# A fused attention and gated-MLP kernel: new order at the front, at the switch and at the tail, and a halved score tile ordered through VectorE with its second half earlier

## The chip, the cores and the metric

The kernel runs on one core of a Trainium2 chip. The metric is the device time of one execution in microseconds, the median of several. The engines named below are TensorE (PE; its weight loads are PEld), VectorE (DVE), ScalarE (ACT), GpSimd (POOL) and SyncE (SP, which issues DMAs); each has its own queue of instructions and runs it in order.

## What is computed

`x` is 2048 tokens of 512 features. It is normalised (layer norm without weights). An attention block with 32 heads of 16 features and an MLP with a hidden width of 1376 both read the normalised `x`; the MLP's result, through silu, gates the attention's result, and `x` is added.

```python
def _A_ref(x, wqkv, wo):                       # H = 32, Dh = 16
    qkv = (x @ wqkv).reshape(B, S, 3, H, Dh).transpose(2, 0, 3, 1, 4)
    q, k, v = qkv[0], qkv[1], qkv[2]
    p = softmax(einsum("bhqd,bhkd->bhqk", q, k) * Dh ** -0.5)
    o = einsum("bhqk,bhkd->bhqd", p, v)
    return o.transpose(0, 2, 1, 3).reshape(B, S, D) @ wo
def _B_ref(x, w1, b1, w2, b2):
    return gelu(x @ w1 + b1) @ w2 + b2
xn = layernorm(x)
return x + _A_ref(xn, wqkv, wo) * silu(_B_ref(xn, w1, b1, w2, b2))
```

## The kernel before

**Precision.** Most matmuls run on a rounded format (float32r) and take operands as a high part and a remainder (low part). A product is then three matmuls, high by high, high by low, low by high (`mm3`, L80).

**Row tiles.** The array is used as two row tiles of 64 rows, which run matmuls side by side. One score matmul needs 48 or 50 rows. The kernel never lets both row tiles write one PSUM bank at once: where both write one bank, the second waits until the first has finished.

**Units and heads.** The 32 heads form 8 groups of 4; the tokens form 4 chunks of 512. A unit is one group and one chunk of queries, 32 units in all. Attention runs in two passes. The first finds, per query, the maximum over a group's scores: score matmuls of 128 queries by 512 keys (L183, function `s_mm`) and reductions on VectorE (`s_max`, L189). The second makes scores again, transposed (`t_one`, L732), with the maximum folded in, ScalarE takes the exponential (L734), and the result is multiplied by V and a column of ones (`pv_step`, L797; 8 matmuls, as float32).

**Stages.** At the front (to about 57 us), tokens are loaded, normalised (`ln`: `moments`, `rstd`, `norm`; L418 to L432), transposed and split into high and low (`turn`, `split`, L74 and L75); V and the first two groups of queries and keys follow (`v_tile`, `q_first`). Then, to about 480 us, a plan interleaves the MLP and the other queries and keys (`quad`, `half`, `down`; `quad` makes four V tiles, `half` one row tile's share of two products) with score matmuls of the first pass (`fill`). From there on, a loop over n = 0 to 512 runs both passes: at each n an order string is read, one letter after the other:

- T: one transposed score matmul of the second pass with its exponential; four in each n.
- S: one whole score tile (128 by 512) of the first pass, with its reduction. Successive S take alternate row tiles.
- X and Y: a halved tile. X computes 256 keys of one head on the first row tile into the first half of a bank; Y computes 256 keys of another head on the second row tile into the other half of the same bank; then one reduction covers both. So X and Y must not overlap, and Y's matmul waits for a token.
- V: the eight matmuls of `pv_step` for the step before.

The token is an empty instruction on an engine's queue: it waits for X's matmul, and Y waits for it.

```python
token = nc.gpsimd.nop().ins                                               # L221
tc.add_manual_dep(token, x.name, SYNC, reason="row tile done")
...
tc.add_manual_dep(y, token.name, SYNC, reason="other row tile")
```

Waits are counts on semaphores: a waiting instruction names an engine and how many of its counted instructions must have finished. An instruction that waits holds up those behind it on its queue.

The order is `ORDER[3]` where three score tiles fall due in a step, which is 490 steps in a row; `ORDER[0]` ("TTTTV") where none does. n = 0 and n = 1 have strings of their own. Score tiles of the first pass take three PSUM banks in turn (`s_ring`); X holds its bank until Y's reduction has been asked for (`s_ring.append(pool)` in `s_op`), and a matmul into a bank waits for the reduction that read it last. T takes four other banks in turn, V one.

After the loop comes the tail: the last unit is divided by its sums (`o_move`, `o_den`, `o_div`), token tiles are rounded (`w_token`, `w_chunk`, `w_round`), multiplied by `wo` (`w_mul`, L80), gated and added (`w_gate` L893, `w_add` L898) and stored. T3 are the last four token tiles, 12 to 15; tile 15 is done in two halves of 256 columns.

Of the kernel before, what the change touches and what calls it, by code (L numbers as in the profile page):

```python
# [16 lines left out]
P = 128  # L17
# [19 lines left out]
FILL0 = 38  # L37
HB = 4
W2B = 2
ORDER = {0: "TTTTV", 3: "TXSTTSTYV"}  # L40
HC = CH // 2
PAIRED = 28
KB = 3
# [5 lines left out]
def fused(ctx: ExitStack, tc: tile.TileContext, x, wqk, wv, wo, w1, b1, w2, b2, out):  # L49
# [27 lines left out]
    def mm3(ps, lhs, rhs, first, last, then=None):  # L77
        n = 0
        for a, b in ((0, 0), (0, 1), (1, 0)):
            nc.tensor.matmul(ps, lhs[a], rhs[b], start=first and n == 0, stop=last and n == 2)  # L80
            n += 1
            if then:
                then()
# [42 lines left out]
    def slot(i, shape, dtype=F32):  # L126
        return big.tile(list(shape), dtype, name=f"slot{i}")
# [81 lines left out]
    def s_op(op):  # L209
        if op == "S":  # L210
            if whole:
                s_whole(whole.pop(), 1)
            else:
                whole.append(jobs.pop(0))
                s_whole(whole[0], 0)
        elif op == "X":
            if not cut:
                cut[:] = [jobs.pop(0), 0]
            ps, pool = s_tile(True)
            x = s_mm(ps, cut[0], 0, 0, cut[1] * HC, HC)  # L220
            token = nc.gpsimd.nop().ins  # L221
            tc.add_manual_dep(token, x.name, SYNC, reason="row tile done")
            cut[2:] = [ps, pool, token]
            run_off()
        else:
            job, n, ps, pool, token = cut
            y = s_mm(ps, job, 1, HC, n * HC, HC)
            tc.add_manual_dep(y, token.name, SYNC, reason="other row tile")
            s_max(ps, job, slice(0, 2), n)
            s_ring.append(pool)  # L230
            cut[1] += 1
            if n:
                cut.clear()
# [76 lines left out]
            pairs.append([("q", g, c), ("q", g, c + 1)])  # L310
    parts = [(c, f, h) for c in range(NCH) for f in range(FT) for h in range(2)]
    is_m = [pair[0][0] == "m" for pair in pairs]
    plan, nd = [("first", g) for g in range(VQ - 1)], 0
    for j in range(len(pairs)):
        for h in range(2):
            plan.append(("half", j, h))
            if j == 0 and h == 1:
                plan.append(("first", VQ - 1))
            ready = 4 * sum(is_m[:j])
            due = next((i for i in range(j, len(pairs)) if is_m[i]), len(pairs))  # L320
            nxt = next((i for i in range(j + h, len(pairs)) if is_m[i]), len(pairs))
            left = 2 * (nxt - j) + 1 - h
            need = 4 * sum(is_m[:nxt]) - 4 - nd
            room = 2 * (due + 1 - j) - h
            n = 2 if nd < len(parts) and parts[nd][2] and ready - nd > room else 1
            n = max(n, need - 2 * (left - 1))
            while nd < ready and n > 0:
                c, f, k = parts[nd]
                if f == 0 and k == 0 and plan[-1][0] == "down":
                    break  # L330
                plan.append(("down", parts[nd]))
                nd += 1
                n -= 1
# [58 lines left out]
    with ExitStack() as s1:  # L392
# [4 lines left out]
        def a_tile(shape):  # L397
            banks[0] += 1
            i = banks[0] % 6
            if i < 3:  # L400
                return (ps_a, ps_b, ps_x)[i].tile(list(shape), F32, name="ps")
            return ps_t.tile(list(shape), F32, name="pst")
# [48 lines left out]

        def q_first(c):
            pq = {}
            for g in range(2):
                ps = pq["q", g, c] = a_tile((P, CH))
                for k in range(KT):
                    ks = slice(k * P, (k + 1) * P)
                    mm3(ps, (W1[g][0][:, ks], W1[g][1][:, ks]), (xh[c][:, k], xl[c][:, k]), k == 0, k == KT - 1)
            evac(list(pq), pq)

        for t in range(4):
# [39 lines left out]
        def wv_low(k):  # L501
            nc.gpsimd.tensor_sub(wv_l[:, k], wv_r[:, k], wv_h[:, k].bitcast(F32))
# [5 lines left out]
            turn(t)  # L508
        for k in range(KT):
            nc.scalar.activation(wv_h[:, k], wv_r[:, k], AF.Copy)  # L510
        for k in range(KT - 1):
            wv_low(k)
        ln(NCH, NCH)
        consts()
        pool_after(2 * NCH - 1)
        wv_low(KT - 1)
        q_first(0)
        for c in range(1, NCH):
            for t in range(NCH * c, NCH * c + NCH):
# [21 lines left out]
        qzs.append(qzp.tile([P, 2, CH], F32R, name=f"qz{i}"))  # L541

    load_qs(0)
    load_k(0, c0=0, n=S - CH)
    v_tile(NCH - 2)
    q_first(NCH - 1)
    v_tile(NCH - 1)
# [144 lines left out]
            run((terms(y, 0, False), terms(x, 1, False)), {2: [lambda: w1_load(j + 2), errand], 10: [chore]})  # L692
            evac((x, y), PH)

    def quad(n):
        us = first[n]
        for u, b in zip(us, BANKS[n]):
            pool, name = {"x": (ps_x, "ps"), "m": (ps_m, "ps"), "v": (ps_v, "pv"), "t": (ps_t, "pst")}[b]
            PH[u] = pool.tile([P, CH], F32, name=name)
        for i in range(4):  # L700
            hooks = {6: [mark]} if i in (1, 2) else {}
            if n == VQ - 2 and i in (0, 2):
                hooks[3] = [lambda: w1_split(0) if i == 0 else w1_load(1)]
            run((terms(us[i], 0, i < 2), terms(us[(i + 2) % 4], 1, i < 2)), hooks)
            if i >= 2:
                for u in (us[i - 2], us[i]):
                    v_out(u[1] * NCH + u[2], PH.pop(u))
# [29 lines left out]
    for n, e in enumerate(plan):  # L737
        if e[0] == "half":
            half(*e[1:])
        elif e[0] == "first":  # L740
            quad(e[1])
            if e[1] == 0:
                ask_qs(1)
        else:
            if e[1] == parts[-2]:
                nc.scalar.activation(mhw, ident_r[:1, :1].bitcast(F32), AF.Exp)
            if e[1] == parts[-1]:
                for i in range(EARLY):
                    t_one(0, 0, i // 2, i % 2)
            down(*e[1])  # L750
        if e == ("first", VQ - 1):
            w2_split(0)
            w2_load(2)
            ask_k(1)
        if e[0] == "half" and pairs[e[1]][0] == ("q", NG - 1, 0) and e[2] == 1:
            kts.append([slot(p, (P, S), F32R) for p in range(2)])
            kws.append(None)
            qss.append(slot(2, (P, 2, 2, CH), F32R))
            ask_k(2)
        if n == len(plan) - 8:  # L760
            load_qt(0)
            load_mh(0)
# [46 lines left out]
    def o_rows(u, j):  # L809
        g, c = divmod(u, NCH)  # L810
        r0 = 64 * (g % 2) + DH * j
        return slice(r0, r0 + DH), c, g // 2
# [10 lines left out]
    def o_den(u):  # L823
        dr = DR.pop(u)
        nc.vector.reciprocal(dr, dr)
        nc.sync.dma_start(den_d[u].rearrange("j (a i) -> (j a) i", i=GH * CH // P), dr)
        DN[u] = wb.tile([P, CH], F32, name="dn", bufs=1)
        for j in range(GH):
            nc.sync.dma_start(DN[u][o_rows(u, j)[0]], den_d[u, j:j + 1].to_broadcast([DH, CH]))

    def o_div(u, eng):
        g, c = divmod(u, NCH)
# [25 lines left out]
        nc.vector.scalar_tensor_tensor(g, e, 1.0, g, op0=OP.add, op1=OP.mult)  # L858

    def w_round(blocks, src, lo):  # L860
        oh = wb.tile([P, KT, P], F32R, name="oh", bufs=3)
        ol = wb.tile([P, KT, P], F32R, name="ol", bufs=3)
        n = len(blocks)
        nc.scalar.activation(oh[:, :n], src, AF.Copy)
        lo.tensor_sub(ol[:, :n], src, oh[:, :n].bitcast(F32))
        for i, b in enumerate(blocks):
            OTS[b] = (oh[:, i], ol[:, i])
# [28 lines left out]
    def w_add(t, eng, i=0):  # L896
        gx, cs = GX[t], cols(t)[i]
        eng.tensor_add(gx[:, 0, cs], gx[:, 0, cs], gx[:, 1, cs])  # L898
        nc.sync.dma_start(out[t * P:(t + 1) * P, cs], gx[:, 0, cs])

    def w_out(t, eng):
        w_gate(t)
        w_add(t, eng)
# [50 lines left out]
    for n in range(L + 1):  # L954
        ua, ka = divmod(n, 16)
        want = due(n) - due(n - 1)
        i = 0
        for op in ORDER[want] if n > 1 else ("TTTTV", "TTTVTSS")[n]:
            if op in "SXY":
                s_op(op)  # L960
            elif op == "V":
                if n:
                    pv_step(*divmod(n - 1, 16))
                for _ in range(4):
                    tick()
                flush()
            else:
                if EARLY <= 4 * n + i < 4 * L:
                    t_one(ua, ka, i % 2, 1 - i // 2)
                for f, args in todo.get((n, i), []):  # L970
                    f(*args)
                i += 1
# [4 lines left out]
    w_out(late[0], nc.gpsimd)  # L977
    w_chunk(1, nc.gpsimd)
    w_mul(late[1], KS)
    w_out(late[1], nc.gpsimd)  # L980
    w_chunk(2, nc.gpsimd)
    for k in KS[:-1]:
        for t in T3:
            w_mul(t, (k,))
    o_div(NU - 1, nc.vector)
    w_chunk(KT - 1, nc.vector)
    ends = [(t, i) for t in T3 for i in range(len(cols(t)))]
    for n, (t, i) in enumerate(ends):
        w_mul(t, KS[-1:], (i,))
        w_gate(t, i)  # L990
        if n == 0:
            w_add(t, nc.gpsimd)
        elif n > 1:
            w_add(*ends[n - 1][:1], nc.vector, ends[n - 1][1])
    w_add(ends[-1][0], nc.vector, ends[-1][1])


# [31 lines left out]
```

## Time and profile before

| | |
|---|---|
| three runs | 1602.58, 1604.39, 1605.58 us |
| median | 1604.39 us |
| profiled execution, its own time | 1603.36 us |
| its span in the profile | 1601.6 us |
| instructions in it | 32363 |

The profile is of one execution. Times in it are microseconds from the start of the span unless marked ns. A row of the time line has the start, the length, the engine, the line of the kernel, the operation, what is written and read, the shapes, how many like it were merged (x3), and in brackets how long the engine was idle before and what ended that. A "q" behind an engine is its sequencer: waits and DMA issues, which do not count as busy time. Ends of matmuls are modelled. Line numbers are those of the kernel before; behind the change they are up to five higher.

### The profile page before, as it was taken

The numbers are of one execution on the slowest core, as the hardware profiler recorded it, in microseconds if no ns is written. First come the engines' busy times: TensorE is split into PE (matmuls) and PEld (weight loads), VectorE is DVE, ScalarE is ACT, GpSimd is POOL, SyncE is SP. The second block draws the span as 40 slices with busy tenths as digits, with TensorE's granted clock in tenths as the row PEclk, the third lists the DMA queues.
The fourth block names the chain that finished last, engine by engine and source line by source line (L and its number), as shares of the span: only waits on it lengthen the run. The fifth ranks groups of instructions, "written<-read, shape, count | busy, mean of one in ns | idle before, by whom it ended". The sixth has DMA issues, their size and how long they took to land.

```text
span 1601.6 us, 32363 instructions
## 1 busy us (share of the span) xinstructions
PE 1590.1 (99%) x12132; PEld 914.8 (57%) x12132; DVE 1380.9 (86%) x2257; ACT 1260.4 (79%) x2521; POOL 377.7 (24%) x398
## 2 busy tenths in 40 slices
PE   9999999999999999999999999999999999999998
PEld 7889899999994444444444444444444444444445
DVE  7489898989888999999999989999999999999743
ACT  4333443434349999999999999999999999999984
POOL 4135575756640001000100200100010000000144
PEclk9999999999999999999999999999999999999999
DMA  6625343454331113111410311321141111110252
GB/s 204 149 58 149 118 136 97 152 142 134 113 98 55 40 31 68 29 37 42 80 32 25 69 41 29 60 40 28 31 73 27 31 29 39 32 30 21 62 199 89
DMA packets 76286, 116.92 MB, mean 73 GB/s; under 512 B 24836, under 2 KB 26116, under 8 KB 74952
## 3 DMA queue, kind: packets, MB, share of 16 engines
q1 hardware_dynamic: 72668, 102.42, 22.7%
q0 software_dynamic: 3264, 12.35, 3.9%
q8 instruction: 96, 1.57, 0.4%
q14 instruction: 62, 0.51, 0.1%
q10 hardware_dynamic: 196, 0.07, 0.0%
HBM read 84.35 MB, written 25.97 MB: 69 GB/s over the span
## 4 chain that ended last, share of the span: by engine, by line
PE 97%; DVE 1%; DMA 0%; ACT 0%; issue 0%; SPq 0%; DVEq 0%; ACTq 0%
PE pv L797 32%; PE ps L183 18%; PE pst L732 16%; PE ps L583 12%; PE pst L583 7%; PE ps L732 5%; PE ps L80 3%; PE pv L583 2%; PE pst L80 1%; DVE slot L75 0%; DMA xt<-in_x 0%; DVE st L418 0%; DVE xn L432 0%; DVE slot L893 0%; ACT hh L377 0%
## 5 line engine op out<-in xcount | busy, mean ns | idle before, releaser
L189 DVE TENSOR_REDUCE mx<-ps 128x2 f32<-128x512 f32 x2048 | 1299.1, 685 | 152.9 <-PE ps L183 87.6
L734 ACT ACTIVATE slot<-pst 128x512 f32<-128x512 f32 x1533 | 833.8, 612 | 22.1 <-PE ps L732 8.9
L797 PE MATMUL pv<-slot,vsb 128*32 128x512 f32 x4096 | 545.3, 605 | 0.0
L183 PE MATMUL ps<-kt,slot 48*128 48x512 f32 (+1 forms) x1364 | 393.4, 376 | 0.0
L732 PE MATMUL pst<-qt,kt 50*128 50x512 f32 x1149 | 372.8, 430 | 0.5 <-DVE gt L665 0.4
L732 PEld LDWEIGHTS pst<-qt,kt 50*128 50x128 f32 x1149 | 178.9, 184 | 279.7 <-ACT slot L734 264.0
L734 ACT ACTIVATE slot<-ps 128x512 f32<-128x512 f32 x515 | 315.3, 613 | 4.4 <-PE ps L732 1.2
L183 PEld LDWEIGHTS ps<-kt,slot 48*128 48x128 f32 x1364 | 210.8, 184 | 34.7 <-DVE mx L189 22.1
L583 PE MATMUL ps<-slot,w1h 64*128 64x512 f32 x1088 | 218.5, 393 | 0.4 <-ACT junk L597 0.4
L183 PE MATMUL ps<-kt,qz 48*128 48x512 f32 x512 | 213.0, 416 | 0.0
L183 PE MATMUL ps<-slot,slot 48*128 48x512 f32 (+1 forms) x598 | 172.5, 376 | 0.7 <-DVE mx L189 0.7
L732 PE MATMUL ps<-qt,kt 50*128 50x512 f32 x387 | 162.4, 422 | 0.0
L583 PEld LDWEIGHTS ps<-slot,w1h 64*128 64x128 f32 x1088 | 152.1, 185 | 7.4 <-ACT junk L597 1.7
L797 PEld LDWEIGHTS pv<-slot,vsb 128*32 128x32 f32 x4096 | 80.6, 108 | 120.3 <-issue 112.2
L583 PE MATMUL ps<-slot,w1l 64*128 64x512 f32 x544 | 142.3, 393 | 0.0
L378 POOL TENSOR_TENSOR hl<-hg,hh 128x512 fp32r<-128x512 f32 x76 | 96.8, 1295 | 121.5 <-ACT hh L377 84.7
L597 ACT ACTIVATE junk<-ident_r 1x1 f32<-1x1 f32 x93 | 18.2, 196 | 124.8 <-PE pst L583 120.2
L732 PE MATMUL pst<-qt,slot 50*128 50x512 f32 x384 | 112.6, 416 | 0.0
L251 POOL CAST nmh<-nm 128x16 fp32r<-128x16 f32 x32 | 6.3, 197 | 414.6 <-PE ps L183 111.5
L183 PEld LDWEIGHTS ps<-kt,qz 48*128 48x128 f32 x512 | 93.7, 183 | 16.5 <-issue 0.4
L183 PEld LDWEIGHTS ps<-slot,slot 48*128 48x128 f32 x598 | 92.2, 184 | 17.1 <-DVE mx L189 11.4
L732 PEld LDWEIGHTS ps<-qt,kt 50*128 50x128 f32 x387 | 71.0, 184 | 44.0 <-ACT slot L734 42.8
(150 smaller groups left out, 1711.1 us busy)
## 6 DMA issues: line engine op xcount, KB each, us to landing
raw<-in_w SPq DMA_DIRECT2D x88, 256.0 KB
qk_h<-hh SPq DMA_DIRECT2D x32, 256.0 KB
qk_l<-hl SPq DMA_DIRECT2D x32, 256.0 KB
qt<-qk_h SPq DMA_DIRECT2D x128, 64.0 KB
slot<-qk_h SPq DMA_DIRECT2D x92, 64.0 KB
xt<-in_x SPq DMA_DIRECT2D x16, 256.0 KB
g_d<-gt POOLq DMA_DIRECT2D x16, 256.0 KB, 3.4
qt<-qk_l SPq DMA_DIRECT2D x64, 64.0 KB
```

The source lines that it names most:

```text
L80: nc.tensor.matmul(ps, lhs[a], rhs[b], start=first and n == 0, stop=last and n == 2)
L183: return nc.tensor.matmul(ps[:, c0:c0 + w], QS[u][r, p, qi * P:(qi + 1) * P], kts[u // NCH % KB][p][r, k0:k0 + w], start=True, stop=True).ins
L189: nc.vector.tensor_reduce(MX[u][:, 2 * p:2 * p + 2, qi, ki][:, heads, parts], ps.rearrange("p (n c) -> p n c", c=HC), axis=AX.X, op=OP.max)
L251: nc.gpsimd.tensor_copy(hl[:, 0], nm)
L378: nc.gpsimd.tensor_sub(hl, raw, hh.bitcast(F32))
L583: i = nc.tensor.matmul(ps, lhs[r], rhs[r], start=first, stop=last).ins
L597: i = nc.scalar.activation(junk[:, :1], ident_r[:1, :1].bitcast(F32), AF.Copy).ins
L732: nc.tensor.matmul(ps, kts[g % KB][p][r, k * P:(k + 1) * P], QT[u][r, p, :], start=True, stop=True)
L734: nc.scalar.activation(PT[u, k][:, 2 * p + a, :], ps, AF.Exp, scale=SCALE)
L797: nc.tensor.matmul(PV[u][32 * j:32 * j + 32, :], vsb[:, k, h:h + 32], PT[u, k][:, j, :], start=(k == 0), stop=(k == NT - 1))
```

## The change

Front: `q_first` runs all high-by-high products of its two groups first, then high by low part of x, then low part of the weights. The last two of four subtractions for the low part of V's weights (`wv_low`, on POOL) come after the second `ln` instead of the last one. The first load of K takes columns 0 to 511 and then 512 to 1535 instead of all 1536 at once. The third quad is cut in two and stands around the second half of the first pair.

Switch: the string for n = 1 is "TTSTSVT" instead of "TTTVTSS".

The step: the empty instruction is on VectorE's queue instead of POOL's, and the order string of a step with three tiles has Y ahead of the second S and of the last T.

Tail: the sums of a unit come back in one broadcast load instead of four; the last rounding has a buffer of its own; tile 15 is multiplied as a whole at the very end; all last adds are on VectorE.

```diff
-ORDER = {0: "TTTTV", 3: "TXSTTSTYV"}
+ORDER = {0: "TTTTV", 3: "TXSTTYTSV"}
...
-            token = nc.gpsimd.nop().ins
+            token = nc.vector.nop().ins
...
-    plan, nd = [("first", g) for g in range(VQ - 1)], 0
+    plan, nd = [("first", g, i) for g in range(VQ - 1) for i in (0, 2)], 0
...
-            if j == 0 and h == 1:
-                plan.append(("first", VQ - 1))
+            if j == 0:
+                plan.append(("first", VQ - 1, 2 * h))
...
-            for g in range(2):
-                ps = pq["q", g, c] = a_tile((P, CH))
-                for k in range(KT):
-                    ks = slice(k * P, (k + 1) * P)
-                    mm3(ps, (W1[g][0][:, ks], W1[g][1][:, ks]), (xh[c][:, k], xl[c][:, k]), k == 0, k == KT - 1)
+            for n, (i, j) in enumerate(((0, 0), (0, 1), (1, 0))):
+                for g in range(2):
+                    if n == 0:
+                        pq["q", g, c] = a_tile((P, CH))
+                    for k in range(KT):
+                        nc.tensor.matmul(pq["q", g, c], W1[g][i][:, k * P:(k + 1) * P], (xh, xl)[j][c][:, k],
+                                         start=n == 0 and k == 0, stop=n == 2 and k == KT - 1)
...
-        for k in range(KT - 1):
+        for k in range(KT - 2):
             wv_low(k)
         ln(NCH, NCH)
         consts()
         pool_after(2 * NCH - 1)
-        wv_low(KT - 1)
+        for k in range(KT - 2, KT):
+            wv_low(k)
...
-    load_k(0, c0=0, n=S - CH)
+    load_k(0, c0=0, n=CH)
+    load_k(0, c0=CH, n=S - 2 * CH)
...
-        for j in range(GH):
-            nc.sync.dma_start(DN[u][o_rows(u, j)[0]], den_d[u, j:j + 1].to_broadcast([DH, CH]))
+        r0 = o_rows(u, 0)[0].start
+        nc.sync.dma_start(DN[u][r0:r0 + GH * DH],
+                          den_d[u].rearrange("j (o c) -> j o c", o=1).to_broadcast([GH, DH, CH]))
...
+        if blocks == [(t, KT - 1) for t in T3]:
+            both = slot(3 + len(PN) % 3, (P, 4, KT, P), F32R)
+            oh, ol = both[:, 0], both[:, 1]
+        else:
...
-        for op in ORDER[want] if n > 1 else ("TTTTV", "TTTVTSS")[n]:
+        for op in ORDER[want] if n > 1 else ("TTTTV", "TTSTSVT")[n]:
...
-    w_out(late[1], nc.gpsimd)
+    w_out(late[1], nc.vector)
...
-        for t in T3:
+        for t in T3[:-1]:
             w_mul(t, (k,))
...
-        w_mul(t, KS[-1:], (i,))
+        w_mul(t, KS[-1:] if t < NT - 1 else KS, (i,))
         w_gate(t, i)
-        if n == 0:
-            w_add(t, nc.gpsimd)
-        elif n > 1:
-            w_add(*ends[n - 1][:1], nc.vector, ends[n - 1][1])
-    w_add(ends[-1][0], nc.vector, ends[-1][1])
+        w_add(t, nc.vector, i)
```

More of the change, by code (lines that the diff above doesn't have):

```diff
@@ L693, in half, with quad @@
             evac((x, y), PH)
-    def quad(n):
+    def quad(n, at):
         us = first[n]
-        for u, b in zip(us, BANKS[n]):
+        for u, b in zip(us, BANKS[n]) if at == 0 else ():
             pool, name = {"x": (ps_x, "ps"), "m": (ps_m, "ps"), "v": (ps_v, "pv"), "t": (ps_t, "pst")}[b]
             PH[u] = pool.tile([P, CH], F32, name=name)
-        for i in range(4):
+        for i in range(at, at + 2):
             hooks = {6: [mark]} if i in (1, 2) else {}
@@ L740, in fused @@
         elif e[0] == "first":
-            quad(e[1])
-            if e[1] == 0:
+            quad(*e[1:])
+            if e[1:] == (0, 2):
                 ask_qs(1)
@@ L750, in fused @@
             down(*e[1])
-        if e == ("first", VQ - 1):
+        if e == ("first", VQ - 1, 2):
             w2_split(0)
@@ L860, in w_round @@
     def w_round(blocks, src, lo):
-        oh = wb.tile([P, KT, P], F32R, name="oh", bufs=3)
-        ol = wb.tile([P, KT, P], F32R, name="ol", bufs=3)
+        if blocks == [(t, KT - 1) for t in T3]:
+            both = slot(3 + len(PN) % 3, (P, 4, KT, P), F32R)
+            oh, ol = both[:, 0], both[:, 1]
+        else:
+            oh = wb.tile([P, KT, P], F32R, name="oh", bufs=3)
+            ol = wb.tile([P, KT, P], F32R, name="ol", bufs=3)
         n = len(blocks)
```

## The prediction

> **What bounds the kernel now.** I read the page first, then the empty instruction's own line, then the weight loads of TensorE in order of time.
>
> ```profile
> span 1601.6 us, 32363 instructions
> PE 1590.1 (99%) x12132; PEld 914.8 (57%) x12132; DVE 1380.9 (86%) x2257; ACT 1260.4 (79%) x2521; POOL 377.7 (24%) x398
> L221 POOLq EVENT_SEMAPHORE  x490: 17/17/17, 483.2 to 1510.4; - x164
> 1000.00:1040.00 40.00, 40.00 (x308) 17.16 (x309) 36.82 (x61) 39.69 (x79) 4.28 (x8) 1.00 0.29 57
> ```
>
> The third row is the empty instruction: 490 of them, one in each step that has a halved tile, from 483.2 to 1510.4 us. So these steps take (1510.4 - 483.2) / 489 = 2.10 us each and fill 1027 of 1602 us. In the fourth row (one 40 us window: TensorE, its weight loads, VectorE, ScalarE and POOL busy for 40.00, 17.16, 36.82, 39.69 and 4.28) ScalarE looks full and TensorE too, so no engine total says what a step waits for. Two steps in a row do. Weight loads, start and length; T is L732, S is L183, V is L797:
>
> ```profile
> 945.16 0.18 PEld L732 LDWEIGHTS pst<-qt,kt 50*128 50x128 f32 x1 [0.84 <-ACT slot L734]
> 945.17 0.18 PEld L183 LDWEIGHTS ps<-kt,slot 48*128 48x128 f32 x1
> ...
> 945.63 0.18 PEld L183 LDWEIGHTS ps<-kt,slot 48*128 48x128 f32 x1
> 945.68 0.18 PEld L732 LDWEIGHTS ps<-qt,kt 50*128 50x128 f32 x1
> 945.80 0.18 PEld L183 LDWEIGHTS ps<-kt,slot 48*128 48x128 f32 x1
> 946.18 0.16 PEld L797 LDWEIGHTS pv<-slot,vsb 128*32 128x32 f32 x8 [0.20 <-issue]
> 947.18 0.18 PEld L732 LDWEIGHTS pst<-qt,kt 50*128 50x128 f32 x1 [0.84 <-ACT slot L734]
> ...
> 947.77 0.18 PEld L183 LDWEIGHTS ps<-kt,slot 48*128 48x128 f32 x1 [0.17 <-DVE mx L189]
> ...
> 948.32 0.16 PEld L797 LDWEIGHTS pv<-slot,vsb 128*32 128x32 f32 x8 [0.25 <-issue]
> 949.31 0.18 PEld L732 LDWEIGHTS pst<-qt,kt 50*128 50x128 f32 x1 [0.84 <-ACT slot L734]
> ```
>
> Measured from a step's first X (945.17): the second S loads at 0.46, the fourth T at 0.51, Y at 0.63, V at 1.01, and the next step begins 1.00 after V: 2.01 us. In the next step the second S loads only at 0.59, released by VectorE, V starts 0.55 after it, and the step takes 2.13. The reductions say why:
>
> ```profile
> 944.30 1.28 DVE L189 TENSOR_REDUCE mx<-ps 128x2 f32<-128x512 f32 x2
> 944.90 0.68 DVE L189 TENSOR_REDUCE mx<-ps 128x2 f32<-128x512 f32 x1
> 945.83 2.70 DVE L189 TENSOR_REDUCE mx<-ps 128x2 f32<-128x512 f32 x4 [0.25 <-PE ps L183]
> ```
>
> The second row is the latter of the pair in the first, seen alone: reductions follow at 0.60. The first of a step starts at 945.83, the third ends at 945.83 + 0.60 + 0.60 + 0.68 = 947.71, and 0.06 later the second S of the next step loads: it writes the bank that the third reduction (of the halved tile) frees. A short step makes the next wait and a long one does not, so 2.01 and 2.13 alternate with mean 2.07; unit boundaries and other work on VectorE make that 2.10. Today Y's token holds Y to 0.63, but Y is last and its row tile is busy until then, so the token costs almost nothing.
>
> **The change part by part.**
>
> *The step, TXSTTSTYV to TXSTTYTSV, 490 times.* Removed: the second S no longer waits for the halved tile. With Y ahead of it that tile's bank goes back earlier, the second S takes over its own bank of the step before, stands last, and its wait (0.53 + 0.06 = 0.59 after X at a step of 2.01, 0.43 at 2.17) lies before its turn. Added: Y is now sixth of eight, and the fourth T, the second S and V are queued behind its wait for the token. What is late next is therefore the token. When does it come?
>
> ```profile
> 945.17 0.49 PE L732 MATMUL pst<-qt,kt 50*128 50x512 f32 x1
> 945.70 1.58 ACT L734 ACTIVATE slot<-pst 128x512 f32<-128x512 f32 x3
> 949.32 0.39 PE L183 MATMUL ps<-kt,slot 48*128 48x256 f32 x1
> ```
>
> X runs beside the first T. X's own end is 0.39 after its start, the first T's 0.49 (945.66). The token waits for a count of finished matmuls, and the first T stands before X in that count, so it cannot pass before 0.49. From there to Y's weight load (0.63) it takes 0.14 through POOL. Through VectorE the two crossings are priced by other rows: TensorE to a waiting engine 0.04 (945.66 to the exponential at 945.70), VectorE to a weight load 0.06 (947.71 to 947.77), so at least 0.10: Y loads at 0.59. The upper end is POOL's 0.63. I take 0.62, nearer POOL's row because that is the same kind of instruction. VectorE's queue does not add to it: the reduction ahead of the empty instruction ends at 0.53 after X in steps of 2.01 and earlier in longer ones, and the one behind it starts only at 0.66 (945.83).
>
> These rows cannot tell a token that follows X alone at 0.39 with a slow POOL from one that follows the first T at 0.49. Here the Trainium skill speaks against the change: its page "TensorE: Matmul & The Clock Gate", section "The mechanism", says that packed matmuls are strictly first in, first out in their ends as well as their starts, so a short X does not finish ahead of a longer T before it. By that rule the token stays behind the T and the step is as below; without it, rival B.
>
> From Y's load on, its row tile still has one half and one whole score matmul to run, then V. That is what followed the gated second S in the long step (a whole one, then a half), and there V came 0.55 later. So a step is 0.62 + 0.55 + 1.00 = 2.17 (2.14 to 2.18 by the bounds), against 2.10: +0.07 x 489 = +34 us (+20 to +39). I set 2.17 against the mean of 2.10, not against 2.07: what delays single steps today (other VectorE work, late exponentials) ends inside the longer wait. If it comes on top instead, 0.03 x 489 = 15 us more.
>
> *Front.* Rows of the first 90 us:
>
> ```profile
> 13.62 0.19 PEld L80 LDWEIGHTS pst<-slot,w1h 128*128 128x128 f32 x1 [0.86 <-DVE slot L75]
> 13.85 3.81 POOL L502 TENSOR_TENSOR kt<-wv_r,kt 128x512 fp32r<-128x512 f32 x3
> 16.81 0.88 DVE L423 TENSOR_SCALAR ve<-mv 128x4 f32<-128x4 f32 x1
> 27.16 0.17 DVE L423 TENSOR_SCALAR ve<-mv 128x4 f32<-128x4 f32 x1
> 51.77 1.41 SPq L109 DMA_DIRECT2D kt<-qk_h  x2
> 54.64 0.41 SPq L109 DMA_DIRECT2D kt<-qk_l  x1
> 34.72 0.19 PEld L80 LDWEIGHTS ps<-slot,w1h 128*128 128x128 f32 x1 [0.48 <-DVE slot L75]
> 83.36 0.30 PEld L583 LDWEIGHTS ps<-slot,w1h 64*128 64x128 f32 x4 [0.80 <-ACT junk L597]
> ```
>
> With all high-by-high products first, TensorE does not need the low half of x at 13.62: at a normal pitch of 0.2 some 0.8 us go. They stay gone only if the next normalised tiles come as much earlier; the 0.88 beside 0.17 of the same instruction, ending with POOL's three subtractions (17.66), says they do, as only two stand before it now: 0.7 to 0.8 us. At 34.72, and in the last such block, which is ordered alike, 0.2 each. A quad between the two halves of the first pair hides the token of 83.36: 0.4 to 0.5. The split load of K issues twelve DMAs on SP where there were six, ahead of four writes of q, the last K columns and the next weights; six took from 51.77 to 55.05, so those slip by up to 3.3 us. They have some 25 us of TensorE's work before the halves of 83.36 as cover: nothing, and +3 without it. Front: -1.6 us (-2.5 to +2).
>
> *Switch.*
>
> ```profile
> 483.10 0.69 DVE L189 TENSOR_REDUCE mx<-ps 128x2 f32<-128x512 f32 x1 [1.66 <-PE ps L732]
> 483.85 0.18 PEld L183 LDWEIGHTS ps<-slot,slot 48*128 48x128 f32 x1 [0.99 <-DVE mx L189]
> 484.63 0.18 PEld L183 LDWEIGHTS ps<-slot,slot 48*128 48x128 f32 x1 [0.50 <-DVE mx L189]
> ```
>
> The two S of step 1 now stand ahead of V, so VectorE starts in its 1.66 idle us and the waits of 0.99 and 0.50 shrink to the normal 0.2: -0.8 us (-1.2 to 0).
>
> *Tail.*
>
> ```profile
> 1578.41 5.77 PE pst L80 x24
> 1589.09 0.89 DVE L865 TENSOR_TENSOR ol<-ot,oh 128x512 fp32r<-128x512 f32 x1 [0.83 <-ACT oh L864]
> 1594.73 0.69 DVE L893 SCALAR_TENSOR_TENSOR slot<-ps,slot 128x512 f32<-128x512 f32 x1
> 1595.34 0.68 DVE L898 TENSOR_TENSOR slot<-slot 128x512 f32<-128x512 f32 x1
> 1595.13 0.28 PE L80 MATMUL pst<-wo_h,ol 128*128 128x256 f32 x1
> 1597.21 0.75 DVE L898 TENSOR_TENSOR slot<-slot 128x256 f32<-128x256 f32 x2
> ```
>
> TensorE's last matmul ends at 1595.41 either way. But its last 24, of half width (24 x 0.12 = 2.9 us), now all belong to the last token tile, so the three other tiles are ready one after the other until 1592.5, and their gates and adds on VectorE (0.61 + 0.60 each) are done by 1595. After the last matmul remain one gate and one add of half width (0.75) and a backlog of some 0.3: 1596.5 instead of 1597.96, -1.5 us (-1.8 to 0). The last rounding, ready at 1589.98 today, is wanted after 27 more matmuls at 0.24, at 1584.18 + 6.5 = 1590.7; one broadcast load for four brings it earlier.
>
> Sum: 34 - 1.6 - 0.8 - 1.5 = +30 us on the profiled execution's 1603.4 (span 1601.6 plus 1.8 around it), which lies 1.0 below the median of the three: 1633.4.
>
> **The rivals.**
>
> B, faster: the token follows X alone, at 0.39 + 0.14 = 0.53. Step 2.08, 0.02 x 489 = -10, with the rest -14: 1589. It decides from a load of Y before 0.55, where the step is 2.10. For it: POOL's answer is otherwise slower than the 0.10 of other engines. Against: the count includes the first T.
>
> C, no change: the token through VectorE is quicker than any crossing shown, Y at 0.55 to 0.56: the step is level, and the small parts are eaten by the queue of SP: about 1604.
>
> D, slower still: the empty instruction passes through VectorE itself, behind the reduction (0.53 at 2.01, later with any other VectorE instruction in front) and pays both crossings: Y at 0.65, step 2.20, +49: 1648. The reduction ends earlier in longer steps, which speaks against it. The Trainium skill, "VectorE: DVE Perf Modes", section "Two Vector instructions with no wait between them", separates a NOP that the sequencer handles alone from an engine NOP that reaches the engine; by the first kind D falls. POOL's row reads POOLq, the sequencer; of VectorE no row of before shows the kind.
>
> **How the numbers follow.** Forecast 0.72, 1618 to 1645 by its own bounds (20 less 5.5, 39 plus 2); D 0.11; B 0.13; C 0.04. 0.2%, 3 us, is what a measurement of this kernel tells from no change. Slower 0.83, same 0.04, faster 0.13. The range starts at 1608, a token halfway between the early bound of 0.59 and the level 0.55, and ends at 1646, short of D's 1648; B and C stay outside.
>
> **What would show it.** After the change: the empty instruction on VectorE's queue, first to last 489 x 2.17 = 1061 us apart; Y's load 0.59 to 0.63 after X, waiting; no more wait of S on VectorE in the steps; no alternation; ScalarE and VectorE less busy per us. The front's wait at 13.62 and the one at 83.36 gone, the 0.88 down to 0.17, the last add 1.1 us after the last matmul. Wrong if Y loads before 0.55.

## The result and the profile after

The changed kernel takes 1644.83 us (median of four executions, 1644.59 to 1645.12) against 1603.99 us for the kernel before (four, 1602.58 to 1605.58). The ratio is 1.0257, 95% interval 1.0243 to 1.0271: 2.6% slower. The profiled execution took 1644.59 us, and its span is 41.2 us longer than that of before (1642.8 less 1601.6).

First the head of the page of the changed kernel:

```profile
span 1642.8 us, 32221 instructions
PE 1634.7 (100%) x12132; PEld 902.2 (55%) x12132; DVE 1382.5 (84%) x2259; ACT 1268.6 (77%) x2520; POOL 374.7 (23%) x396
```

The empty instruction's own line, with who waited for it (us in all, times):

```profile
L221 DVEq EVENT_SEMAPHORE  x490: 21/21/21, 480.2 to 1552.3; - x164
  PEld ps L183: 111.9, 488
```

And the same window of 40 us as before (TensorE, weight loads, VectorE, ScalarE, POOL):

```profile
1000.00:1040.00 40.00, 40.00 (x295) 15.90 (x291) 34.55 (x56) 38.17 (x75) 1.28 (x1) 1.00 0.07 19
```

The empty instruction's row is the reading that matters: a step takes (1552.3 - 480.2) / 489 = 2.192 us where it took 2.101. The row under it is new: weight loads waited for the empty instruction 488 times, 0.23 us each. The window shows the same from the other engines: VectorE and ScalarE work less per microsecond (34.55 and 38.17 where 36.82 and 39.69 stood), so neither sets the pace. The busy time of TensorE grew by 44.6 us with not one matmul more: a busy TensorE here is a waiting one.

One step of the changed kernel, weight loads with start and length; T is now L736, its exponential L738, V L801:

```profile
946.86 0.18 PEld L736 LDWEIGHTS pst<-qt,kt 50*128 50x128 f32 x1 [0.84 <-ACT slot L738]
946.87 0.18 PEld L183 LDWEIGHTS ps<-kt,slot 48*128 48x128 f32 x1
...
947.51 0.18 PEld L183 LDWEIGHTS ps<-kt,slot 48*128 48x128 f32 x1 [0.23 <-DVEq L221]
947.51 0.18 PEld L736 LDWEIGHTS ps<-qt,kt 50*128 50x128 f32 x1
947.62 0.19 PEld L183 LDWEIGHTS ps<-kt,slot 48*128 48x128 f32 x1
948.06 0.16 PEld L801 LDWEIGHTS pv<-slot,vsb 128*32 128x32 f32 x8 [0.25 <-issue]
949.05 0.18 PEld L736 LDWEIGHTS pst<-qt,kt 50*128 50x128 f32 x1 [0.84 <-ACT slot L738]
```

VectorE's reductions in this step and the one before:

```profile
945.35 1.89 DVE L189 TENSOR_REDUCE mx<-ps 128x2 f32<-128x512 f32 x3 [0.29 <-PE ps L183]
947.55 1.89 DVE L189 TENSOR_REDUCE mx<-ps 128x2 f32<-128x512 f32 x3 [0.31 <-PE ps L183]
```

From X (946.87): Y loads at 0.64, waiting; the fourth T is queued behind it (0.64), then the second S (0.75), V at 1.19, and the next step begins 0.99 later. Steps no longer alternate, and no S waits for VectorE, which idles 0.3 in each step. The reduction ahead of the empty instruction ends at 945.35 + 1.89 = 947.24, 0.37 after X.

The small parts. Of the kernel before, for the front the first and last start of two groups of weight loads (transposes of normalised tokens, and the MLP's second product), for the switch V of n = 1 and of n = 2:

```profile
L441 PEld LDWEIGHTS pst<-ident,xn x40: 138/140/143, 10.7 to 41.3; 128*128 128x128 f32 x40
L583 PEld LDWEIGHTS pst<-w2h,hh x264: 182/185/189, 103.7 to 478.6; 64*128 64x128 f32 x132
481.33 0.16 PEld L797 LDWEIGHTS pv<-slot,vsb 128*32 128x32 f32 x8 [0.25 <-issue]
485.18 0.16 PEld L797 LDWEIGHTS pv<-slot,vsb 128*32 128x32 f32 x8 [0.25 <-issue]
```

The same of the changed kernel, and the instruction of VectorE that took 0.88 at 16.81:

```profile
16.40 0.17 DVE L423 TENSOR_SCALAR ve<-mv 128x4 f32<-128x4 f32 x1
L441 PEld LDWEIGHTS pst<-ident,xn x40: 138/140/143, 10.3 to 39.8; 128*128 128x128 f32 x40
L587 PEld LDWEIGHTS pst<-w2h,hh x264: 182/185/192, 101.0 to 475.9; 64*128 64x128 f32 x132
478.55 0.16 PEld L801 LDWEIGHTS pv<-slot,vsb 128*32 128x32 f32 x8 [0.25 <-issue]
481.15 0.16 PEld L801 LDWEIGHTS pv<-slot,vsb 128*32 128x32 f32 x8 [0.24 <-issue]
```

0.4 are there at the first transpose already, ahead of what the change touches; 1.5 by the last, and 2.7 by the first load of the second product. The 2.7 then stay to the end of the stage, over 375 us. The 0.88 is down to 0.17. The switch gave 1.25 (V to V 2.60 instead of 3.85). In the tail, TensorE's wait, its last matmul and VectorE's last add:

```profile
1628.71 0.40 PE L80 MATMUL ps<-wo_l,oh 128*128 128x512 f32 x1
1629.29 0.50 PE L80 MATMUL ps<-wo_h,ol 128*128 128x512 f32 x1 [0.18 <-POOL ol L874]
1637.93 0.28 PE L80 MATMUL pst<-wo_h,slot 128*128 128x256 f32 x1
1639.25 0.42 DVE L907 TENSOR_TENSOR slot<-slot 128x256 f32<-128x256 f32 x1
```

The last add ends 1.46 after the last matmul, where it was 2.55 (1597.96 less 1595.41). But TensorE now waits once for POOL's rounding: two matmuls 0.58 apart instead of 0.23.

The whole, by the empty instruction's first and last row: 3.0 less before the first (483.2 to 480.2), 44.9 more up to the last (1072.1 against 1027.2), 0.7 less behind it (91.2 to 90.5): 41.2. Part of the switch's gain lies in the middle term: from the first empty instruction to V of its step there are 0.95 (480.2 to 481.15) where there were 1.98 (483.2 to 485.18). Without this 1.0 the steps grew by 45.9.

### The profile page after: what moved, and what is told of

The parts are those of the page before. It is cut to its first block, busy times and chain, and to the rows that moved or that the text cites. A ratio compares the mean times of both kernels' runs of the same rounds, so it can differ in the third digit from the quotient of the medians.

```text
span 1642.8 us, 32221 instructions
## 1 busy us (share of the span) xinstructions
PE 1634.7 (100%) x12132; PEld 902.2 (55%) x12132; DVE 1382.5 (84%) x2259; ACT 1268.6 (77%) x2520; POOL 374.7 (23%) x396
## 4 chain that ended last, share of the span: by engine, by line
PE 96%; issue 2%; DVE 1%; POOL 1%; DMA 0%; ACT 0%; POOLq 0%; SPq 0%; DVEq 0%
PE pv L801 30%; PE ps L183 20%; PE pst L736 15%; PE ps L587 12%; PE pst L587 7%; PE ps L736 5%; PE pv L587 2%; PE ps L80 2%; PE ps L459 1%; POOL ol L874 0%; PE pst L80 0%; POOL gx L907 0%; DMA xt<-in_x 0%; DVE st L418 0%; PE pst L441 0%
## 5 line engine op out<-in xcount | busy, mean ns | idle before, releaser
L738 ACT ACTIVATE slot<-pst 128x512 f32<-128x512 f32 x1533 | 835.1, 608 | 49.4 <-PE ps L736 9.6
L801 PE MATMUL pv<-slot,vsb 128*32 128x512 f32 x4096 | 545.2, 605 | 0.0
L183 PE MATMUL ps<-kt,slot 48*128 48x256 f32 (+1 forms) x1364 | 419.1, 387 | 0.0
L736 PE MATMUL pst<-qt,kt 50*128 50x512 f32 x1149 | 377.6, 435 | 0.5 <-DVE gt L669 0.3
L736 PEld LDWEIGHTS pst<-qt,kt 50*128 50x128 f32 x1149 | 178.3, 184 | 274.8 <-ACT slot L738 259.4
L738 ACT ACTIVATE slot<-ps 128x512 f32<-128x512 f32 x515 | 313.1, 609 | 14.0 <-PE ps L736 1.3
L183 PEld LDWEIGHTS ps<-kt,slot 48*128 48x128 f32 x1364 | 201.2, 184 | 77.8 <-DVEq L221 77.7
L183 PE MATMUL ps<-slot,slot 48*128 48x256 f32 (+1 forms) x598 | 184.6, 388 | 0.0
L736 PE MATMUL ps<-qt,kt 50*128 50x512 f32 x387 | 166.1, 431 | 0.0
L801 PEld LDWEIGHTS pv<-slot,vsb 128*32 128x32 f32 x4096 | 80.6, 108 | 130.6 <-issue 122.9
L736 PE MATMUL pst<-qt,slot 50*128 50x512 f32 x384 | 114.0, 424 | 0.0
L183 PEld LDWEIGHTS ps<-slot,slot 48*128 48x128 f32 x598 | 88.6, 184 | 34.3 <-DVEq L221 34.1
L736 PEld LDWEIGHTS ps<-qt,kt 50*128 50x128 f32 x387 | 71.0, 184 | 39.0 <-ACT slot L738 38.0
```

Of the source, the lines that this page charges most:

```text
L183: return nc.tensor.matmul(ps[:, c0:c0 + w], QS[u][r, p, qi * P:(qi + 1) * P], kts[u // NCH % KB][p][r, k0:k0 + w], start=True, stop=True).ins
L736: nc.tensor.matmul(ps, kts[g % KB][p][r, k * P:(k + 1) * P], QT[u][r, p, :], start=True, stop=True)
L738: nc.scalar.activation(PT[u, k][:, 2 * p + a, :], ps, AF.Exp, scale=SCALE)
L801: nc.tensor.matmul(PV[u][32 * j:32 * j + 32, :], vsb[:, k, h:h + 32], PT[u, k][:, j, :], start=(k == 0), stop=(k == NT - 1))
```

## The experiments

Ten kernels; times are medians, ratios are against the kernel before on the same chip (1602.8 to 1603.7 us there).

**Which of the two edits of the step costs it?** Three kernels that make a square with the changed one: new or old order, VectorE or POOL. Front, switch and tail stay changed in all.

```diff
-            token = nc.vector.nop().ins
+            token = nc.gpsimd.nop().ins
```

> The changed kernel with the empty instruction back on POOL; the new order and the edits at front, switch and tail stay. Theory (the order costs it: Y now stands where the fourth T, the second S and V queue behind the token, and the token cannot pass before the first T is counted as done, on whatever engine it runs): Y's weight load stays at 0.63 to 0.65 after X, the step at 2.18 to 2.20 us, the time at 1640 to 1645. Rival (VectorE's own queue holds the empty instruction): on POOL, 23% busy over the span and nearly idle here, Y loads at 0.55 or earlier, the step falls to 2.10 and the time to about 1600.

Measured: 1641.19 us, ratio 1.0237 (1.0222 to 1.0252). Empty instruction, X and Y of one step:

```profile
L221 POOLq EVENT_SEMAPHORE  x490: 17/17/17, 480.1 to 1549.0; - x164
947.28 0.18 PEld L183 LDWEIGHTS ps<-kt,slot 48*128 48x128 f32 x1
947.91 0.18 PEld L183 LDWEIGHTS ps<-kt,slot 48*128 48x128 f32 x1 [0.22 <-POOLq L221]
```

The step is 1068.9 / 489 = 2.186, Y at 0.63 and waiting. The order costs nearly all of it; the rival that VectorE's queue holds the token falls, and the expectation came true.

```diff
-ORDER = {0: "TTTTV", 3: "TXSTTYTSV"}
+ORDER = {0: "TTTTV", 3: "TXSTTSTYV"}
```

> The changed kernel with the order of before, TXSTTSTYV; the empty instruction stays on VectorE, the edits at front, switch and tail stay. Theory (the token is only wanted at 0.63 when Y's row tile is free, so it is hidden again): short and long steps alternate, 2.10 us in the mean, and the time is that of before less the 3.7 us that front, switch and tail gave in the changed kernel's trace (3.0 before the first empty instruction, 0.7 behind the last): 1600, 1598 to 1602. Rival (the token through VectorE costs in itself): Y loads at 0.65 or later here too, V with it, and the time is 1605 or more.

Measured: 1603.53 us, 1.0000 (0.9990 to 1.0010). With both lines of the step put back:

> The changed kernel with the whole step of before: the order TXSTTSTYV and the empty instruction on POOL. What is left of the change is front, switch and tail. Theory: the step is 2.10 us as before, 3.0 us go before the first empty instruction and 0.7 behind the last: 1600, 1599 to 1601, and within 1 us of the kernel with the old order and the token on VectorE. Rival (the three edits cost something in the steps, by what their transfers meet): 1603 or more.

Measured: 1598.77 us, 0.9969 (0.9957 to 0.9981). So front, switch and tail alone make it faster (2.8 less before the first empty instruction, 1.1 behind the last), a little more than expected. The expectation for the old order on VectorE missed, and with it that the two kernels lie within 1 us: the token's engine costs 4.8 us there, though the profile names no load that waits for the token. The old order on VectorE: the empty instruction's row; weight loads of X of three steps in a row, with the second S of the middle one; and, from another stretch, the weight load of X and the reductions of a step:

```profile
L221 DVEq EVENT_SEMAPHORE  x490: 21/21/21, 480.5 to 1511.4; - x164
726.95 0.18 PEld L183 LDWEIGHTS ps<-kt,slot 48*128 48x128 f32 x1
...
728.97 0.18 PEld L183 LDWEIGHTS ps<-kt,slot 48*128 48x128 f32 x1
...
729.57 0.18 PEld L183 LDWEIGHTS ps<-kt,slot 48*128 48x128 f32 x1 [0.19 <-DVE mx L189]
...
731.11 0.18 PEld L183 LDWEIGHTS ps<-kt,slot 48*128 48x128 f32 x1
...
906.06 0.18 PEld L183 LDWEIGHTS ps<-kt,slot 48*128 48x128 f32 x1
906.74 1.89 DVE L189 TENSOR_REDUCE mx<-ps 128x2 f32<-128x512 f32 x3 [0.18 <-PE ps L183]
```

The same rows with the token on POOL:

```profile
L221 POOLq EVENT_SEMAPHORE  x490: 17/17/17, 480.4 to 1506.8; - x164
725.61 0.18 PEld L183 LDWEIGHTS ps<-kt,slot 48*128 48x128 f32 x1
...
727.62 0.18 PEld L183 LDWEIGHTS ps<-kt,slot 48*128 48x128 f32 x1
...
728.20 0.18 PEld L183 LDWEIGHTS ps<-kt,slot 48*128 48x128 f32 x1 [0.17 <-DVE mx L189]
...
729.74 0.18 PEld L183 LDWEIGHTS ps<-kt,slot 48*128 48x128 f32 x1
...
905.69 0.18 PEld L183 LDWEIGHTS ps<-kt,slot 48*128 48x128 f32 x1
906.35 1.89 DVE L189 TENSOR_REDUCE mx<-ps 128x2 f32<-128x512 f32 x3 [0.21 <-PE ps L183]
```

The steps are 2.108 and 2.099 in the mean. The reduction starts 0.68 after X on VectorE and 0.66 on POOL. It stands behind the empty instruction in VectorE's queue, and by the trace it follows the start of that at 0.107 us in nine steps of ten (106 to 108 ns from the 5th to the 95th percentile of 490), while on POOL it does not (79 to 95 ns apart). In the old order VectorE's reductions end in the wait of the second S, so the 0.02 reaches the step, but only the long ones. As before the change, short and long steps alternate in both kernels through most of the loop: by the rows of X 2.02 and 2.14 on VectorE, 2.01 and 2.12 on POOL, and in the long one the waiting S loads 0.60 and 0.58 after X. Half of 0.02 over 489 steps is 4.9 us; the empty instruction's rows differ by 4.5 (1030.9 against 1026.4).

**What is in the delay of VectorE?** Two kernels with the old order: a second empty instruction on VectorE that waits for nothing, right behind the token; and the token on POOL, with an empty instruction without a wait on VectorE in its place.

```diff
             tc.add_manual_dep(token, x.name, SYNC, reason="row tile done")
+            nc.vector.nop()
```

> The kernel with the old order and the token on VectorE, with a second empty instruction, which waits for nothing, right behind the first on VectorE. Theory (an empty instruction that VectorE passes just ahead of the moment at which its reduction is released delays that reduction): the first reduction of a step starts a further 0.01 to 0.02 later than 0.676 after X, and the time goes up again, to 1606 to 1609. Rival (the 4.8 us of VectorE's token came from its answer to TensorE, not from its queue): nothing changes, 1603 to 1604.

Measured: 1602.97 us, 0.9999 (0.9989 to 1.0008).

```diff
+            nc.vector.nop()
-            token = nc.vector.nop().ins
+            token = nc.gpsimd.nop().ins
```

> The kernel with the old order and the token on POOL, with an empty instruction on VectorE that waits for nothing at the place in its queue where the token would stand. Theory (the delay comes from VectorE passing it just ahead of the reduction, because it waits for X): without a wait it is passed as soon as the reduction ahead of it is issued, the first reduction starts at 0.657 after X, and the time is that of the whole old step, 1598 to 1600. Rival (any empty instruction in VectorE's queue costs it 0.02): the first reduction starts at 0.67 or later and the time is 1602 or more.

Measured: 1598.51 us, 0.9968 (0.9957 to 0.9980). The first of these two missed, and its rival had the time about right; the second came as expected. Adding the instruction without a wait costs nothing. But it leaves no row in either trace (both have 32213 instructions, as without it), so whether VectorE passes it for nothing or never gets it stays open. If it never gets it, these two kernels repeat the two before them. So that the delay comes from the wait is not shown; shown is that the token on VectorE, which does wait, brings it: the reduction follows at 0.107.

**Does the first T hold the token?** X goes ahead of the first T; Y stays where the change put it. Token on VectorE.

```diff
-ORDER = {0: "TTTTV", 3: "TXSTTYTSV"}
+ORDER = {0: "TTTTV", 3: "XTSTTYTSV"}
```

> The changed kernel with X ahead of the first T: XTSTTYTSV. Everything else stays, so Y stands as far back as in the changed kernel. Theory (the count that releases the token includes the first T only because T stands before X): X is counted at its own end, 0.39 after its start, the token passes about 0.14 to 0.15 later, Y loads 0.53 to 0.55 after X, the step is 2.10 us or less and the time 1603 or less, down to 1575 if X also starts ahead of T. Rival (the token follows X alone, and 0.64 is what two crossings cost): Y stays at 0.63 to 0.65 after X; the time is 1640 to 1645, less only what X starts ahead of T.

Measured: 1588.89 us, 0.9908 (0.9893 to 0.9923). One step:

```profile
L221 DVEq EVENT_SEMAPHORE  x490: 21/21/21, 480.7 to 1496.5; - x164
902.28 0.18 PEld L183 LDWEIGHTS ps<-kt,slot 48*128 48x128 f32 x1 [0.84 <-DVE mx L189]
902.29 0.18 PEld L736 LDWEIGHTS pst<-qt,kt 50*128 50x128 f32 x1
...
902.78 0.18 PEld L183 LDWEIGHTS ps<-kt,slot 48*128 48x128 f32 x1
902.90 0.18 PEld L736 LDWEIGHTS ps<-qt,kt 50*128 50x128 f32 x1
902.90 0.18 PEld L183 LDWEIGHTS ps<-kt,slot 48*128 48x128 f32 x1
903.33 0.16 PEld L801 LDWEIGHTS pv<-slot,vsb 128*32 128x32 f32 x8 [0.25 <-issue]
904.33 0.18 PEld L183 LDWEIGHTS ps<-kt,slot 48*128 48x128 f32 x1 [0.84 <-DVE mx L189]
```

X and T still load together (902.28, 902.29), and Y loads 0.50 after X instead of 0.64. V follows Y by 0.55 as in the changed kernel, and the regular step is 2.04 to 2.05 (2.077 in the mean with the ends of units). In the trace the median from X's matmul to the empty instruction is 0.569 in the changed kernel and 0.425 here: all of the gain lies ahead of the token, in the count it waits for. The theory came true, with Y a little earlier than the 0.53 to 0.55 expected; the rival, 0.64 as the price of two crossings, falls. The two letters are worth 56 us (1644.83 less 1588.89).

The same with the token on POOL, and with the first late token tile's add moved from POOL to VectorE in the tail (the change had left this one add on POOL):

```diff
-    w_out(late[0], nc.gpsimd)
+    w_out(late[0], nc.vector)
```

> The kernel with X ahead of the first T, with the empty instruction back on POOL; and the first late token tile is added on VectorE too, so that POOL's second rounding in the tail is not behind that add. Two theories of what the empty instruction costs on VectorE in the old order, where nothing waits for it (1603.5 against 1598.8). Theory 1 (it delays the first reduction behind it in VectorE's queue: that starts at 0.676 after X with it, at 0.657 without): here a reduction of the halved tile is the first and VectorE idles 0.15 ahead of it, so the step stays within 0.01 of 2.077 and the time within 1584 to 1589. Theory 2 (the answer itself comes later through VectorE): Y loads 0.02 or more earlier than 0.50 and the time is 1580 or less. In the tail TensorE's wait of 0.58 for POOL's rounding (0.18 of it with nothing running) goes, 0.35 us.

Measured: 1587.17 us, 0.9902 (0.9885 to 0.9918), the fastest of all. Its step is 2.076 against 2.077, so here the token's engine costs almost nothing (0.5 us of the 1.7): on VectorE, too, the empty instruction starts over 0.2 us ahead of the next reduction. Theory 1 came true. TensorE's wait in the tail is gone.

**Is Y ahead of the second S worth anything?** X first, but Y last, as before the change (token on POOL, the same tail):

```diff
-ORDER = {0: "TTTTV", 3: "XTSTTYTSV"}
+ORDER = {0: "TTTTV", 3: "XTSTTSTYV"}
```

> As the kernel with X first, the token on POOL and VectorE's add in the tail, but with the second S ahead of Y as before the change: XTSTTSTYV. It tells whether Y ahead of the second S is worth something once the token comes early. Theory (the halved tile is reduced last again and its bank is the one that the second S of the next step takes): the second S waits for VectorE to about 0.55 to 0.60 after X, short and long steps alternate, 2.09 to 2.10 us in the mean, and the time is 1594 to 1599. Rival (only X ahead of T brings the gain): the step is 2.08 or less and the time 1584 to 1590.

Measured: 1597.72 us, 0.9964 (0.9950 to 0.9978).

```profile
905.53 0.18 PEld L183 LDWEIGHTS ps<-kt,slot 48*128 48x128 f32 x1 [0.84 <-DVE mx L189]
...
907.56 0.18 PEld L183 LDWEIGHTS ps<-kt,slot 48*128 48x128 f32 x1 [0.84 <-DVE mx L189]
...
908.13 0.18 PEld L183 LDWEIGHTS ps<-kt,slot 48*128 48x128 f32 x1 [0.16 <-DVE mx L189]
...
909.67 0.18 PEld L183 LDWEIGHTS ps<-kt,slot 48*128 48x128 f32 x1 [0.84 <-DVE mx L189]
```

The second S waits for VectorE again, 0.57 after X (the third row), in every other step: 2.03 and 2.11 alternate. (The 0.84 at X stands behind V at the first load of a step in the other kernels too, whatever releaser the row names.) So Y's new place is worth 10.5 us (1597.72 less 1587.17), once the token comes in time.

**Can the token be hidden altogether?** X last ahead of V, its Y early in the next step (what changes in `s_op` is that Y is left out until there is an X to finish; in the last such step both stand in it; the loads of the maxima that follow, `load_mh`, come one step later; neither of these is in the diff here):

```diff
-ORDER = {0: "TTTTV", 3: "TXSTTYTSV"}
+ORDER = {0: "TTTTV", 3: "TYSTTSTXV", 4: "TYSTTXTSYV"}
```

> X stands last ahead of V and its Y second in the next step: TYSTTSTXV, the token passes while V runs, through POOL; the tail as in the kernel with X first and the token on POOL. Theory (the token's way of 0.64, or 0.50 with X first, is all that sets the time from X to V): nothing waits for the token, V loads 0.85 to 1.0 after the first T, the step falls to 1.95 to 2.03, then bounded by ScalarE (four exponentials at 0.48 to 0.49 are 1.94): 1540 to 1570. Rival (the halved tile is held longer, and the waits of S on VectorE for banks come back in its place): PEld waits on reductions again and the step is 2.05 to 2.10: 1575 to 1600.

Measured: 1899.72 us, 1.1851 (1.1834 to 1.1869). Both expectations missed. Weight loads of one step:

```profile
900.88 0.29 PEld L183 LDWEIGHTS ps<-kt,slot 48*128 48x128 f32 x2
...
902.27 0.18 PEld L183 LDWEIGHTS ps<-kt,slot 48*128 48x128 f32 x1 [0.75 <-DVE mx L189]
...
903.58 0.18 PEld L734 LDWEIGHTS ps<-qt,slot 50*128 50x128 f32 x1 [0.84 <-ACT slot L736]
```

VectorE in the same step:

```profile
901.53 1.89 DVE L189 TENSOR_REDUCE mx<-ps 128x2 f32<-128x512 f32 x3 [0.82 <-PE ps L183]
```

No load in it waits for the token, as meant (one in the whole run does). But X (902.27) waits 0.75 for the first reduction of its own step, which ends at 901.53 + 0.68 (the length of a reduction seen alone): that of Y. With three banks, three tiles a step and one held over V, the bank that X needs is the one that Y has just filled. The rival named the right wait and was far off in size: 2.7 us a step instead of 2.1. With X two places earlier (TYSTTXTSV):

> As the kernel with Y in the next step, with X two places earlier and the second S last: TYSTTXTSV. Theory: the token has 0.3 us more and was hidden anyway, so the time is that of the other within 5 us, with the difference set by which bank's reduction ends last; no wait for the token in either. Rival (the token was still late there): this one is faster by 10 us or more.

Measured: 1955.33 us, 1.2199 (1.2181 to 1.2217). Both expectations missed here too: it is 56 us slower, and the second S, the last load of a score tile ahead of V, waits for that reduction. By this account a fourth bank would be needed; it was not tried.

## Why the prediction held

The time lies inside the range, near its upper end: the sum gave 1633.4 for the profiled execution, which took 1644.59. The steps gave +45.9 where +34 were put down, and the small parts together -4.7 where -3.9 were (0.4 of them ahead of anything that the change touches).

**The step.** The mechanism was right in each part of the step. Y's load waits (0.23 us, 488 times), the fourth T, the second S and V are queued behind it, VectorE's wait of the second S and the alternation are gone, and VectorE and ScalarE idle more. The times from Y to V and from V to the next step came as put down, 0.55 and 1.00.

**The mis-sized term** is the token: 0.62 was taken between 0.59 and 0.63, and it is 0.640, above the upper end. The lower end, two crossings of 0.04 and 0.06 at other rows, did not hold for an empty instruction: from its start to Y's load the trace has 0.071 on VectorE and 0.067 on POOL, and its start lies 0.569 and 0.566 after X. So VectorE is not between POOL and the faster crossings but 0.007 slower than POOL, which is 3.4 us over the steps and fits the 3.6 between the two kernels. The 0.02 on the term are 10 of the 12 us by which the steps were under-estimated. The rest is small: the regular step is 2.186 and not 0.64 + 0.55 + 1.00 = 2.19, 2 us less; 13 steps at ends of units take 2.40, 3 us more; and the base, without the first of the intervals, in which the switch's gain lies, was 2.098 and not 2.10, 1 us more. The 2.10 of before held as the right base: 40 steps took over 2.3 us before and only 13 do after, so few delays came on top.

**The first T.** That the token waits for the first T, not for X alone, was argued and is now shown: with X first its start moves from 0.569 to 0.425 after X's, with nothing else changed on its way. The Trainium skill, "TensorE: Matmul & The Clock Gate", section "The mechanism", has packed matmuls end in the order in which they start; the trace agrees, by these 0.144 us. The ends that the profile models for the first T and for X, 0.49 and 0.38 after X's start, account for 0.11 of them; where the other 0.03 come from is open. Rival B needed the reverse and falls. Its price was right, in part by luck: with X first Y loads at 0.50 where B had 0.53, which makes the regular step 2.04 instead of 2.08, but ends of units bring the mean back to 2.077, and so the time is 1588.89 where B had 1589.

**Rivals C and D.** C falls with the load at 0.64. D came within 4 us of the time (1648) and to within 0.01 of Y's load (0.65), but not by its mechanism: the reduction ahead of the token ends at 0.37 after X, 0.2 before the token passes, and on POOL, where no reduction can stand ahead of it, the token is as late. Its row reads DVEq, the sequencer.

**The small parts.** The front was put at -1.6 and gave -2.3 behind the first transpose: -1.1 by the last one, about as worked out (0.7 to 0.8 and 0.2), and -1.2 behind it instead of -0.6 to -0.7. The waits at 13.62, 34.72 and 83.36 are gone, and K's split load cost nothing that shows. The switch was put at -0.8 and gave -1.25. The tail was put at -1.5 and gave -0.7. Three things differ from the working. "TensorE's last matmul ends at 1595.41 either way" failed: it ends 18.5 after V's last weight load (1619.72) instead of 18.0 (1577.39). The half-width matmuls of tile 15 had also been the cover of POOL's roundings, and without them TensorE waits 0.35 more; the kernel that moves one more add off POOL has that wait gone and 18.05. The last add ends 1.46 after the last matmul and not 1.1. Against these, the span ends 3.1 after the last add instead of 3.6, which was not in the sum. The other 0.4 lie between the last empty instruction and V's last weight load. That the small parts together lie within 1 us of what was put down is in part luck: front and switch gave more, the tail less.

## What to carry to other kernels

A token's price is set also by what stands ahead of the signalling instruction in the count, not by that instruction alone (0.569 against 0.425 here): put the short one first where order in time is free. Before an instruction is moved forward, compare the time at which its wait ends with its new turn: here it ended just as its turn came, and two places earlier it was 0.23 us late, 488 times. And where banks are few, holding one longer can turn into a wait on the reduction just asked for: 0.75 us a step here.

## What the runs showed of the hardware

An empty instruction with a wait delays what is behind it on its engine after the wait has ended: the reduction started 0.107 us behind its start, and 0.02 later than with the token on POOL. Where the reduction came more than 0.2 after the empty instruction anyway (X first), no such delay shows. The Trainium skill, "Perfetto Trace Analysis", sections "Sequencer-only Instruction (DRAIN, etc)" and "DVE / Act Engine Instruction (TENSOR_ADD, Activation, etc)", has the sequencer hold such an instruction through its wait and fetch the next one only then, while an ordinary one waits in a queue of its own; the fixed distance agrees with that, and 0.086 of it (0.107 less the 0.021 of the row) would then be the price of starting afresh, an estimate. No kernel here separates the wait from the empty instruction itself. It cost 4.8 us where reductions set the step and at most 0.5 where they came 0.2 us later.
